# Attention with decay and a gated feed-forward: two groups of small matmuls move into the visits of their neighbours

## The chip, the cores and the metric

The kernel runs on one core of a Trainium2 chip. Its time is the device time of one execution in microseconds (us); the number that counts is the median of several runs. Five engines work side by side, each with its own queue that runs in order: PE (TensorE, matrix products; PEld is its weight load), DVE (VectorE), ACT (ScalarE), POOL (GpSimd) and SP (SyncE, which issues most of the DMAs). Engines wait for each other by semaphores. PE writes only to PSUM, which has eight banks; DVE and ACT read them.

## The reference: what is computed

For 4 batches and 8 heads, sequences of 768 tokens with 64 numbers each are worked in blocks of 64 tokens. Each block takes its own tokens' scores and a state that is carried from block to block; the result goes through a two-layer network with a cosine gate.

```python
for b in range(nb):                                   # 12 blocks of 64 tokens
    intra = einsum('bhic,bhjc->bhij', qb, kb) * Dmask # scores, decayed and causal
    intra = einsum('bhij,bhjd->bhid', intra, vb)      # values
    inter = einsum('bhid,bhde->bhie', qb * lam_pow, kv_state)   # carried part
    out[block] = intra + inter
    kv_state = lam_block * kv_state + einsum('bhsd,bhse->bhde', kb * rev_pow, vb)
h = x @ w_in                 # x: 3072 x 512, w_in: 512 x 2048
return (h * cos(h)) @ w_out  # w_out: 2048 x 512
```

## The kernel before, in words

**Tokens.** The 3072 tokens are 24 blocks of 128 tokens. Two blocks that stand at the same place of two batches make a pair. The first four blocks are done otherwise, as two "spans" of 256 tokens each, the beginnings of the first two batches. Then come pairs 2 to 11; pair 2, called the third pair here (its number is `SPANS`), is the first one, and it continues the sequences of the two spans. The decays are folded into scaled copies of q and v, so that a state is a plain running sum.

**A pair.** SP loads q, k and v. `prepare` scales q, copies k to bf16 (both into the tile qk) and scales v (v_s). q and k are transposed into qkT, for the third pair on PE (L374) with copies by DVE (L377), for later pairs by DMA (L380). Then `add_scores` plans the scores (L422; DVE multiplies them by a mask into s_m, L427) and the update of the state (L434, in PSUM as ps_kv). `state` (L440) adds the update of each half of a block to the running sum, on DVE, and `state_16` (L445) makes the bf16 copy S on ACT; for the third pair the first sum is written as bf16 at once by DVE. `add_stretch` plans the values (L484, in PSUM as ps_o) and, onto the same bank, the carried part, which multiplies S by the transposed q (L516). Copies out of ps_o give xT (L524), the input of the network.

**Values in two groups.** For a block, the values come from four products of 64x64. `values` emits the first 16 matmuls of a pair (the crosswise ones), `values_carried` the other 16 and then the carried part. Both groups write the same places of PSUM from different row halves of the array[...]. Pairs in `APART` use other banks. Where the next pair's scores and update lie in between, a 1x1 DVE copy (`turn`, L501) reads the first group's result and the second group waits for it. The third pair has neither, and `values_carried` puts a PE drain between the groups:

```python
if not more and not apart:
    nc.tensor.drain()
```

**The spans' state.** `add_span_state` makes the running sum that both spans leave behind: 32 matmuls (L705), a copy from PSUM by DVE (L709), a bf16 copy by POOL (L712). The third pair needs it: the first half of its carried part reads the bf16 copy (the second half reads S), and its S is this sum plus its own update.

**The network.** `add_ffn` plans for each tile of tokens (4, 2, 2, 2, 2, 2, 2, 4 and 4 blocks, `TILES`) the hidden matmuls (L738, ps_h), the cosine on ACT (L744), the product on DVE (L750, g), the output matmuls (L784, ps_f, in fours of 0.216 us each), the copy out on ACT (L798) and the store on SP (L805 for the spans' tokens, L807 after). The weights w_out come in four parts through POOL's DMA queue (L268).

**The order.** Nothing here is ordered by hand. Every step is a `Task` with an engine, an assumed duration, the tasks it depends on and a priority; `Planner.order` plays them forward and gives each engine's order and the PSUM banks. A task's `then` makes another one follow it at once on its engine; scores and update of most pairs are tied like this, for the third pair they aren't (`early`). Tasks with `LATE` (30.0) as priority are taken when little else can start.

Of the kernel before, what the change touches and what calls it, by code (L numbers as in the profile page):

```python
# [18 lines left out]
SPANS = 2  # L19
# [13 lines left out]
OUTS = [{"qT": ("ACT", "ACT"), "kT": ("ACT", "ACT")}, {"qT": ("ACT", "ACT"), "kT": ("ACT", "ACT")}]  # L33
VALUES_OUT = [("ACT", "ACT"), ("DVE", "ACT")]
STATE_OUT = [("ACT", "ACT"), ("ACT", "ACT")]
LATE = 30.0
ORDER = "q0 k0 q1 k1 v0 v1 i0 i1 i2 i3 i4 i5 o0 o1 o2 q4 q5 k4 k5 o3"

W_IN = [2, 2, 2, 4, 4, 2]
# [104 lines left out]
def kernel(  # L144
# [10 lines left out]
    nc = tc.nc  # L155
# [89 lines left out]
    SW = 0.11  # L245
    halves = [slice(i * D, (i + 1) * D) for i in range(2)]
    live = {}
# [4 lines left out]
    def prio_attn(n, part):  # L252
        i = next(i for i in range(len(TILES)) if n < first[i + 1])
        return begins[i - 1] + unit[i - 1] * (n - n % 2 - first[i] + 2 * part) / TILES[i]
# [146 lines left out]
    def new_sum(pr, half):  # L401
        t = live["sum", pr, half] = toks.tile([P, H, D], F32, tag=f"sum{half}", bufs=1 + half, name=f"sum{half}")
        return t
# [66 lines left out]
        qk_head[pr].frees = [T[pr, 0], T[pr, 1], u]  # L470
        return s_t, u

    def add_stretch(pr):

        n0 = 2 * pr
        g, c = divmod(pr, NB)
        pa = lambda part: prio_attn(n0, part)
        tile_i, j0 = tile_of(n0)

        def value(s, half, o=None):  # L480
            m = halves[half]
            o = live["o", n0 + s][:, :, m] if o is None else o
            for h in range(H):
                yield lambda h=h: nc.tensor.matmul(  # L484
                    o[halves[h % 2], h // 2], lhsT=live["v_s", n0 + s][m, h, :], rhs=live["s_m", n0 + s][m, h, :],
                    start=(apart or s != half) and h < 2, stop=True, skip_group_check=True)

        def values(t):
            for s in range(2):
                live["o", n0 + s] = bank(t.bank[s], [P, NP, P], F32, "ps_o")  # L490
            cross = [None, None]
            if apart:

                cross = live["cross", pr] = [bank(i, [P, NP, D], F32, "ps_x") for i in t.bank[2:]]
            for x, y in zip(value(1, 0, cross[0]), value(0, 1, cross[1])):
                x()
                y()

        def turn(_):

            live["turn", pr] = nc.vector.tensor_copy(spare[D:D + 1, 0:1], live["o", n0][D:D + 1, NP - 1, D:D + 1])  # L501

        def values_carried(_):
            if not more and not apart:
                nc.tensor.drain()
            for x, y in zip(value(0, 0), value(1, 1)):
                i = x()
                y()
                if ("turn", pr) in live:
                    tc.add_manual_dep(i.ins, live.pop(("turn", pr)).ins.name, mybir.DependencyInfo(  # L510
                        mybir.DependencyClass.Sync, mybir.DependencyReason.DATA), reason="row halves in turn")
            for half in range(0 if c else 1, 2):
                S = live["S", pr, 0] if half else live["S", pr - 1, 1]
                for h in range(H):
                    for s, r in enumerate(halves):
                        nc.tensor.matmul(live["o", n0 + s][halves[h % 2], h // 2, halves[half]], lhsT=S[r, h, :],  # L516
                                         rhs=live["qkT", pr][r, 0, h, halves[half]],
                                         start=False, stop=True, skip_group_check=True)

        def values_out(_, s, e):  # L520
            if ("xT", tile_i) not in live:
                live["xT", tile_i] = work.tile([P, KD, 4 * P], BF16, tag="xT", name="xT")
            j = j0 + s
            (nc.vector.tensor_copy if e == "DVE" else nc.scalar.copy)(  # L524
                live["xT", tile_i][:, :, j * P:(j + 1) * P], live.pop(("o", n0 + s)))

        def halves_out(_, s, half):
            if ("xT", tile_i) not in live:
                live["xT", tile_i] = work.tile([P, KD, 4 * P], BF16, tag="xT", name="xT")
            o, i = live["o", n0 + s][:, :, halves[half]], (j0 + s) * P + half * D  # L530
            x = live["xT", tile_i][:, :, i:i + D]
            if s == half:
                nc.scalar.copy(x, o)
            elif half or c:
                nc.vector.tensor_add(x, o, live["cross_f", pr][half])  # L535
            else:
                nc.vector.tensor_copy(x, live["cross_f", pr][half])

        def cross_out(_, half):
            live.setdefault(("cross_f", pr), {})[half] = toks.tile([P, NP, D], F32, tag=f"cross{half}", bufs=1, name=f"cross{half}")  # L540
            nc.scalar.copy(live["cross_f", pr][half], live["cross", pr][half])

        deps = [So[n0], So[n0 + 1], Uo[pr, 0], Uo.get((pr - 1, 1)) if c else None]
        more = pr + 1 < NBLK // 2 and pr + 1 not in ALONE
        apart = pr in APART
        v1 = pl.add("PE", 4 * QUART + SW, deps, values, pa(0.5), banks=2 + 2 * apart)
        chain = [v1]
        if more:
            nxt = list(add_scores(pr + 1, pa(0.5)))
            for t in nxt:  # L550
                v1.deps += [d for d in t.deps if d not in nxt]
            chain += nxt
        if more:
            deps = deps + [pl.add("DVE", 0.12, [v1], turn, pa(-9.0))]
        v2 = v12[pr] = pl.add("PE", (12 if c else 8) * QUART + (0.0 if more or apart else 0.28), deps, values_carried, pa(0.5))
        chain.append(v2)
        v1.bank_frees = []
        if apart:
            after = [v2] + ([h_last[tile_i - 2]] if tile_i >= 2 else [])
            copies = [pl.add("ACT", 0.42, after, partial(halves_out, s=s, half=s), pa(0.6)) for s in range(2)]  # L560
            moved = [pl.add("ACT", 0.42, [v1], partial(cross_out, half=half), pa(0.55)) for half in range(2)]
            sums = [pl.add("DVE", 0.4, after + [moved[1 - s]], partial(halves_out, s=s, half=1 - s), pa(0.0 if pr == SPANS else 0.59 - 0.01 * s)) for s in range(2)]
            for s in range(2):
                Vo[n0 + s] = [copies[s], sums[s]]
            v1.bank_frees = [Vo[n0], Vo[n0 + 1], [moved[0]], [moved[1]]]
        for s in range(2):
            So[n0 + s].frees = [v2]
            v_head[n0 + s].frees = [v2]
            if apart:
                continue  # L570
            e = "DVE" if pr == SPANS and s == 0 else "ACT"
            Vo[n0 + s] = [pl.add(e, 0.65, [v2] + ([h_last[tile_i - 2]] if tile_i >= 2 else []), partial(values_out, s=s, e=e),
                                 pa(0.0 if e == "DVE" else 0.6))]
            v1.bank_frees.append(Vo[n0 + s])
        qkT_head[pr].frees = [v2]
        if (pr + 1, 1) in Uo:
            Uo[pr + 1, 1].deps.append(v2)
        for x, y in zip(chain, chain[1:]):
            x.then = y
            y.deps.append(x)  # L580
# [113 lines left out]
        L["update"], L["values"], L["carried"] = u, v0, second  # L694
        L["straight"] = v1

    def add_span_state():


        def update(t):  # L700
            live["kv", 1] = bank(t.bank[0], [P, H, D], F32, "ps_kv")
            for h in range(H):
                for s in range(2):
                    for L, r in zip(spans, halves):
                        nc.tensor.matmul(live["kv", 1][r, h, :], lhsT=L["k"][:, s, h, :], rhs=L["v"][:, s, h, :],  # L705
                                         start=(h == 0 and s == 0), stop=True, skip_group_check=True)

        def state(_):
            nc.vector.tensor_copy(new_sum(1, 1), live["kv", 1])  # L709

        def state_16(_):
            nc.gpsimd.tensor_copy(new_S(1, 1), live["sum", 1, 1])  # L712

        u = pl.add("PE", 16 * QUART + SW, span_deps + [w_t["out", 0]], update, LATE, banks=1)
        x = pl.add("DVE", 0.69, [u], state, LATE)
        Uo[1, 1] = pl.add("POOL", 0.61, [x], state_16, LATE)
        u.bank_frees = [[x]]

    h_last, o_last = {}, {}
# [120 lines left out]
    idle = pl.add("SETUP", 0.0, [], None, -1e9, banks=1)  # L840
    for x in range(SPANS):
        add_span(x)
    add_span_state()
    for pr in range(SPANS, NBLK // 2):
        prepare(pr)
    add_scores(SPANS, prio_attn(2 * SPANS, 0.2))
    pr = SPANS
    for i in range(len(TILES)):
        while 2 * pr < first[i + 1]:
            if pr + 1 in ALONE:  # L850
                add_scores(pr + 1, prio_attn(2 * pr + 2, 0.2))
            add_stretch(pr)
            pr += 1
        add_ffn(i)
    for f in range(2, SPLIT):
# [60 lines left out]
```

## Time and profile before

| | |
|---|---|
| median of 5 runs | 204.26 us (204.19 to 204.32) |
| profiled execution, its own time | 204.56 us |
| its span, first to last instruction | 202.9 us |
| granted TensorE clock | 0.999 |
| PE busy, share of the span | 97% |
| DVE, ACT, POOL busy | 58%, 59%, 32% |
| moved by DMA | 33.94 MB, mean 167 GB/s |

The span is what the trace sees; the execution's own time has 1.66 us more around it. The page gives for each engine its busy time, and the chain that ended last: from the last instruction back, at each step to what released it or to the instruction before it on its engine. The timeline lists instructions in order of start, runs of the same kind merged; the duration of such a run reaches from the first start to the last end, and in brackets stands how long the engine was idle before it and what ended that.

### The profile page before, as it was taken

The page shows a single profiled execution, that of the slowest core. Times are in us where ns is not written, and L with a number is a line of the kernel's source. Part 1 is how long each engine was busy: PE and PEld are TensorE (multiplying, and loading weights), DVE is VectorE, ACT ScalarE, POOL GpSimd, SP SyncE. Part 2 cuts the span into 40 slices and gives each one's busy share as a digit, 9 for nine tenths or more (in the row PEclk, how much of TensorE's full clock was granted, in tenths as well). Part 3 has the DMA queues.
Part 4 walks back from the last instruction along what each step waited for, and adds up shares of the span by engine and source line. Part 5 has one row for each costly group of instructions (what it writes and reads, how often), then busy time and mean ns, then how long its engine had stood idle before and what let it go on. Part 6 is the DMA issues. An engine that isn't in the chain of part 4 may idle for free.

```text
span 202.9 us, 5941 instructions
## 1 busy us (share of the span) xinstructions
PE 196.7 (97%) x2469; PEld 116.6 (57%) x2469; DVE 116.8 (58%) x228; ACT 120.0 (59%) x240; POOL 64.7 (32%) x85
## 2 busy tenths in 40 slices
PE   6799999999999999999999999999999999999994
PEld 3367444547847848666658676755445444444443
DVE  2888774256954967848548675734579544444001
ACT  4978872128837878565639667653877655355120
POOL 5694004046145163643733364552620000000000
PEclk9999999999999999999999999999999999999999
DMA  4999999979889998999999999999940010111112
GB/s 118 323 190 205 203 202 220 195 162 226 192 218 232 244 217 190 225 120 273 239 246 181 169 278 210 247 145 238 249 113 3 3 52 0 52 55 52 52 52 103
DMA packets 96762, 33.94 MB, mean 167 GB/s; under 512 B 84320, under 2 KB 93792, under 8 KB 96736
## 3 DMA queue, kind: packets, MB, share of 16 engines
q1 hardware_dynamic: 89232, 28.78, 63.4%
q0 software_dynamic: 7360, 4.72, 16.3%
q8 instruction: 19, 0.31, 0.6%
q10 hardware_dynamic: 144, 0.07, 0.1%
q14 instruction: 7, 0.06, 0.1%
HBM read 27.27 MB, written 6.29 MB: 165 GB/s over the span
## 4 chain that ended last, share of the span: by engine, by line
PE 93%; DMA 3%; SPq 2%; POOL 1%; issue 0%; ACT 0%; POOLq 0%; ACTq 0%
PE ps_h L738 42%; PE ps_f L784 41%; DMA sp_f<-in_k_dram 3%; PE ps_kv L434 2%; PE ps_o L484 2%; PE ps_s L422 2%; PE ps_o L516 2%; SPq L268 1%; PE ps_o L644 1%; PE ps_kv L631 1%; POOL k_sp L599 1%; PE ps_x L484 0%; PE ps_t L374 0%; PE ps_t L607 0%; PE ps_s L618 0%; PE ps_o L650 0%
## 5 line engine op out<-in xcount | busy, mean ns | idle before, releaser
L750 DVE TENSOR_TENSOR g<-ps_h,cos 128x256 bf16<-128x256 f32 (+1 forms) x148 | 73.2, 503 | 42.8 <-ACT cos L744 42.0
L744 ACT ACTIVATE cos<-ps_h,halfpi 128x256 f32<-128x256 f32 (+1 forms) x148 | 75.7, 539 | 29.4 <-PE ps_h L738 28.6
L784 PE MATMUL ps_f<-w_out_sb,g 128*128 128x512 bf16 (+2 forms) x400 | 91.5, 371 | 0.0
L738 PE MATMUL ps_h<-xT,w_in_sb 128*128 128x256 bf16 (+1 forms) x592 | 91.3, 304 | 0.0
L738 PEld LDWEIGHTS <-w_in_sb 128*128 128x128 bf16 x592 | 57.1, 98 | 30.1 <-DVE xT L524 0.4
L784 PEld LDWEIGHTS <-g 128*128 128x128 bf16 x400 | 37.6, 98 | 37.2
L798 ACT COPY o_sb<-ps_f 128x512 f32<-128x512 f32 (+1 forms) x24 | 13.8, 573 | 30.4 <-PE ps_f L784 30.3
L344 POOL TENSOR_TENSOR qk<-q_f,q_scale 128x512 bf16<-128x512 f32 x19 | 19.6, 1045 | 35.0 <-DMA q_f<-in_q_dram 28.4
L352 POOL TENSOR_TENSOR v_s<-v_f,v_scale 128x512 bf16<-128x512 f32 x19 | 19.6, 1044 | 16.2 <-DMA v_f<-in_v_dram 16.2
L427 DVE TENSOR_TENSOR s_m<-ps_s,mask 128x512 bf16<-128x512 f32 x20 | 13.0, 685 | 3.6 <-PE ps_s L422 3.1
L348 POOL CAST qk<-k_f 128x512 bf16<-128x512 f32 x18 | 11.1, 614 | 12.7 <-DMA k_f<-in_k_dram 12.5
L524 ACT CAST xT<-ps_o 128x512 bf16<-128x512 f32 x11 | 6.0, 588 | 9.6 <-PE ps_o L516 6.2
L440 DVE TENSOR_TENSOR sum<-sum,ps_kv 128x512 f32<-128x512 f32 x15 | 10.2, 681 | 0.6
L445 ACT CAST S<-sum 128x512 bf16<-128x512 f32 x15 | 9.2, 617 | 0.9 <-DVE sum L440 0.8
L798 DVE COPY o_sb<-ps_f 128x384 f32<-128x384 f32 x1 | 0.6, 558 | 11.5 <-DMA out_dram<-o_sb 11.5
L484 PEld LDWEIGHTS <-v_s 64*64 64x64 bf16 x320 | 3.9, 107 | 4.1 <-issue 3.6
L876 PE MATMUL ps_idle<-blank 128*128 128x512 f32 (+2 forms) x8 | 4.7, 725 | 1.6 <-DVE blank L211 1.6
L623 DVE TENSOR_TENSOR s_m_sp<-ps_s,mask_sp 128x512 bf16<-128x512 f32 x8 | 5.1, 684 | 1.0 <-PE ps_s L618 1.0
L484 PE MATMUL ps_o<-s_m,v_s 64*64 64x64 bf16 x256 | 5.1, 196 | 0.1
L712 POOL CAST S<-sum 128x512 bf16<-128x512 f32 x1 | 0.6, 608 | 14.0 <-DVE sum L709 14.0
L501 DVE COPY spare<-ps_o 1x1 f32<-1x1 f32 x5 | 0.8, 156 | 7.3 <-PE ps_o L484 7.3
L535 DVE TENSOR_TENSOR xT<-ps_o,cross 128x256 bf16<-128x256 f32 x8 | 3.1, 422 | 2.9 <-PE ps_o L516 2.9
(74 smaller groups left out, 95.4 us busy)
## 6 DMA issues: line engine op xcount, KB each, us to landing
q_f<-in_q_dram SPq DMA_DIRECT2D x20, 256.0 KB, 4.2
k_f<-in_k_dram SPq DMA_DIRECT2D x20, 256.0 KB, 4.4
v_f<-in_v_dram SPq DMA_DIRECT2D x20, 256.0 KB, 5.0
out_dram<-o_sb SPq DMA_DIRECT2D x19, 256.0 KB, 3.4
w_out_sb<-in_moe_w_out_dram POOLq DMA_DIRECT2D x4, 512.0 KB, 12.6
sp_f<-in_q_dram SPq DMA_DIRECT2D x2, 512.0 KB, 6.3
sp_f<-in_k_dram SPq DMA_DIRECT2D x2, 512.0 KB, 5.7
w_in_sb<-in_moe_w_in_dram POOLq DMA_DIRECT2D x4, 256.0 KB, 6.9
```

The costliest lines, as they stand in the source:

```text
L344: vec[e].tensor_mul(new_qk()[:, 0, :, s], live.pop(("q_f", 2 * pr + s)), q_scale[:, c, :].unsqueeze(2).to_broadcast([P, H, D]))
L348: (nc.scalar.copy if early else nc.gpsimd.tensor_copy)(new_qk()[:, 1, :, s], live.pop(("k_f", 2 * pr + s)))
L352: vec[e].tensor_mul(live["v_s", 2 * pr + s], live.pop(("v_f", 2 * pr + s)), v_scale[:, c, :].unsqueeze(2).to_broadcast([P, H, D]))
L427: nc.vector.tensor_mul(t, live["s", pr][s], mask.unsqueeze(1).to_broadcast([P, H, D]))
L440: nc.vector.tensor_add(new, live["sum", pr, 0] if half else live["sum", pr - 1, 1], live["kv", pr][half])
L445: nc.scalar.copy(new_S(pr, half), live["sum", pr, half])
L484: yield lambda h=h: nc.tensor.matmul(o[halves[h % 2], h // 2], lhsT=live["v_s", n0 + s][m, h, :], rhs=live["s_m", n0 + s][m, h, :], start= ...
L738: nc.tensor.matmul(t[:, :n], lhsT=w_in_sb[:, kd, f * P:(f + 1) * P], rhs=live["xT", i][:, kd, at], start=(kd == 0), stop=(kd == KD - 1))
L744: nc.scalar.activation(c[:, :n], live["h", i, f, at.start][:, :n], AF.Sin, bias=halfpi)
L750: return nc.vector.tensor_mul(live["g", i][:, f, at], live.pop(("h", i, f, at.start))[:, :n], live.pop(("c", i, f, at.start))[:, :n])
L784: nc.tensor.matmul(live["f", i, j, piece][:, :width], lhsT=live["g", i][:, f, j * P:(j + 1) * P], rhs=w_out_sb[:, f, part], start=(f == 0) ...
L798: (nc.scalar.copy if eng == "ACT" else nc.vector.tensor_copy)(o[:, :width], live["f", i, j, piece][:, :width])
```

## The change: what it does

The spans' state update is tied in front of the third pair's scores (`u.then = s_t`), with their priority instead of `LATE`; its copy out of PSUM goes from DVE to ACT. The third pair's first group of values is tied in front of that pair's state update (`v1.then = ahead`), and takes the update's dependencies as well as those on the scores. In `values_carried` the third pair loses the drain and gets the 1x1 copy (`turn`) to wait for. For all later pairs the plan is made by the same lines as before.

On the engines this gives the following. PE, between the hidden matmuls of the first tile and those of the second, before: 32 of the spans' update; 24 output matmuls; 8 transposes; 8 output; 8 transposes; 8 output; 32 scores; 16 output; 32 of the update; 4 output; 32 values with a drain in the middle; 32 carried; 4 output. After: 28 output; 8 transposes; 8 output; 8 transposes; 8 output; 32 of the spans' update; 32 scores; 12 output; 16 values; 32 of the update; 4 output; 16 values; 32 carried; 4 output. DVE loses the copy of the spans' sum and gets the 1x1 copy behind its scaling of v. ACT gets the spans' sum between its last k copy and its first output copy. POOL's bf16 copy moves behind its first scaling of v. On SP two output stores of later tiles change places with one q load each.

```diff
-LATE = 30.0
...
-    def add_stretch(pr):
+    def add_stretch(pr, ahead=None):
...
         def values_carried(_):
-            if not more and not apart:
+            if not more and not apart and not ahead:
                 nc.tensor.drain()
...
-        v1 = pl.add("PE", 4 * QUART + SW, deps, values, pa(0.5), banks=2 + 2 * apart)
-        chain = [v1]
+        if ahead:
+            v1 = pl.add("PE", 4 * QUART + SW, [So[n0], So[n0 + 1]] + ahead.deps, values, ahead.prio, banks=2)
+            v1.then = ahead
+            ahead.deps.append(v1)
+            chain = []
+        else:
+            v1 = pl.add("PE", 4 * QUART + SW, deps, values, pa(0.5), banks=2 + 2 * apart)
+            chain = [v1]
...
-        if more:
+        if more or ahead:
             deps = deps + [pl.add("DVE", 0.12, [v1], turn, pa(-9.0))]
-        v2 = v12[pr] = pl.add("PE", (12 if c else 8) * QUART + (0.0 if more or apart else 0.28), deps, values_carried, pa(0.5))
+        v2 = v12[pr] = pl.add("PE", (12 if c else 8) * QUART + (SW if ahead else 0.0), deps, values_carried, pa(0.5))
...
-    def add_span_state():
+    def add_span_state(s_t, prio):
...
         def state(_):
-            nc.vector.tensor_copy(new_sum(1, 1), live["kv", 1])
+            nc.scalar.copy(new_sum(1, 1), live["kv", 1])
...
-        u = pl.add("PE", 16 * QUART + SW, span_deps + [w_t["out", 0]], update, LATE, banks=1)
-        x = pl.add("DVE", 0.69, [u], state, LATE)
-        Uo[1, 1] = pl.add("POOL", 0.61, [x], state_16, LATE)
+        u = pl.add("PE", 16 * QUART + SW, span_deps + s_t.deps, update, prio, banks=1)
+        u.then = s_t
+        s_t.deps.append(u)
+        x = pl.add("ACT", 0.61, [u], state, prio)
+        Uo[1, 1] = pl.add("POOL", 0.61, [x], state_16, prio)
...
-    add_span_state()
...
-    add_scores(SPANS, prio_attn(2 * SPANS, 0.2))
+    first_scores, first_update = add_scores(SPANS, prio_attn(2 * SPANS, 0.2))
+    add_span_state(first_scores, prio_attn(2 * SPANS, 0.2))
...
-            add_stretch(pr)
+            add_stretch(pr, first_update if pr == SPANS else None)
```

## The prediction, made before the changed kernel ran

> **What bounds the kernel now.** I read the page first: its busy shares and the engines of the chain that ended last.
>
> ```profile
> PE 196.7 (97%) x2469; PEld 116.6 (57%) x2469; DVE 116.8 (58%) x228; ACT 120.0 (59%) x240; POOL 64.7 (32%) x85
> PE 93%; DMA 3%; SPq 2%; POOL 1%; issue 0%; ACT 0%; POOLq 0%; ACTq 0%
> ```
>
> TensorE is on the chain for 93% of the span, and no other engine is above 59% busy. So the time is the length of PE's queue plus what PE stands still, and an edit is worth what it takes off that. All edits lie between 30 and 47 us, so next I read the chain in order of time there (start us, us, what):
>
> ```profile
> 30.11 0.62 PE ps_kv L705 x32
> 30.74 5.29 PE ps_f L784 x24
> ...
> 40.37 0.38 PE ps_s L422 x32
> 40.74 3.56 PE ps_f L784 x16
> 44.30 0.55 PE ps_kv L434 x32
> 44.85 0.97 PE ps_f L784 x4
> 45.82 0.25 PE ps_o L484 x16
> 46.07 0.10 issue
> 46.17 0.32 PE ps_o L484 x16
> 46.49 0.28 PE ps_o L516 x32
> 46.77 0.97 PE ps_f L784 x4
> ...
> 56.48 0.38 PE ps_s L422 x32
> 56.86 0.37 PE ps_kv L434 x32
> 57.23 3.56 PE ps_f L784 x16
> ```
>
> Four times PE leaves the wide output matmuls (ps_f, 128 rows by 128 columns of the array) for small attention matmuls: the spans' state update (L705), the scores (L422), the state update (L434), and the values with the carried part (L484, L516). I call each excursion a visit. The return costs too: 24, 16 and 4 output matmuls at 0.216 us are 5.18, 3.46 and 0.86, and the chain has 5.29, 3.56 and 0.97, so 0.10 to 0.11 more on every return. The visits therefore cost (0.62+0.11) + (0.38+0.10) + (0.55+0.11) + (0.25+0.10+0.32+0.28+0.11) = 2.93 us.
>
> Then the timeline, for array shapes and for what the visits wait on (start us, us, engine, line, operation, tiles, array shape):
>
> ```profile
> 14.51 0.62 PE L631 MATMUL ps_kv<-v_sp,k_sp 64*128 64x128 bf16 x8
> 15.06 0.42 PE L644 MATMUL ps_o<-s_m_sp,v_sp 64*64 64x128 bf16 x16
> ...
> 40.30 0.45 PE L422 MATMUL ps_s<-qkT 64*64 64x64 bf16 x32
> 42.77 1.04 POOL L352 TENSOR_TENSOR v_s<-v_f,v_scale 128x512 bf16<-128x512 f32 x1 [7.41 <-DMA v_f<-in_v_dram]
> 43.38 0.98 DVE L352 TENSOR_TENSOR v_s<-v_f,v_scale 128x512 bf16<-128x512 f32 x1 [1.22 <-DMA v_f<-in_v_dram]
> 44.23 0.61 PE L434 MATMUL ps_kv<-v_s,qk 64*64 64x64 bf16 x32
> 44.89 0.69 DVE L440 TENSOR_TENSOR S<-sum,ps_kv 128x512 bf16<-128x512 f32 x1 [0.53 <-PE ps_kv L434]
> ```
>
> The 32 scores take 0.45 us, the 32 matmuls of the update 0.61. The difference, 0.16, is a stall just after the update's start: its third matmul needs the scaled values that DVE finishes at 43.38+0.98 = 44.36, and those were held by the landing of v_f. The transfer sets this moment, not PE.
>
> **The change, part by part.**
>
> Part A, spans' update into the scores' visit. One return (0.11) and one entry go. What stands in the way is the shape: L705 uses 128*64, the scores 64*64. The Trainium skill (TensorEngine Tiling (Array Packing), section Tiling Modes) says that changing the tiling mode, unlike changing the tile, drains the array; that speaks against the gain. The trace has no 128*64 next to 64*64; the nearest row is L631 (64*128) followed by L644 (64*64): eight matmuls 0.057 apart from 14.51 end their starts at 14.91, and the next starts at 15.06, 0.15 later, 0.09 more than their spacing. Groups of one shape follow each other without it: in other visits 32 scores behind values take 0.26 on the chain (at 104.97). By the rule, scores behind the spans' update cost 0.26 + 0.10 = 0.36; without it 0.26. A is then 0.62+0.36+0.11 = 1.09 against 0.73+0.48 = 1.21: saves 0.12, or 0.22 if this pair of shapes doesn't drain. I take 0.12.
>
> Moved with it: the copy of the span state from PSUM goes from DVE (0.69) to ACT and the bf16 copy on POOL (0.61) comes later. ACT is free: between its two k copies (the last ends at 35.79+0.62 = 36.41) and its first output copy at 43.48 it has nothing, so 0.61 at about 41.0 hides there. On POOL the bf16 copy now stands behind the scaling of v at 42.77 to 43.81, so it ends at 44.42 and holds the next q scaling (44.32 before) by 0.1; POOL idles 0.46 us two operations later (k copy at 46.82, waiting for its load), so this ends there. Its reader, the first half of the carried matmuls, comes at about 46.0: 1.6 us of cover. No load changes its place in POOL's or SP's queue; the last w_out part on POOL waits for q_f and is issued at 33.54 either way. Late on SP two output stores move ahead of one q_f load each (near 90 and 135 us); the copy that feeds the first had ended at 88.42, and the second by 135.02, so neither waits.
>
> The 24 output matmuls of the chain at 30.74 become 28, start 0.72 earlier, and the 16 at 40.74 become 12: no matmul is added or lost. DVE is 0.69 freer at 30.8, where it is ahead of need.
>
> Part B, the first 16 value matmuls into the update's visit. Values first 0.25 (like 45.82), then the update at the price it has behind another group (0.29 at 70.26; 0.37 at 56.86, the upper end), and 0.11 for the return: 0.65, against 0.66 with its stall and 0.50 without. So B adds 0.15 of PE work.
>
> Part C, second values and carried part alone. The drain (0.10 issue, and 0.32 instead of 0.25 for the second group's restart) and the first group go: 0.25+0.28+0.11 = 0.64 against 1.06, saves 0.42; with carried at 0.34, as at 61.16, 0.36. In the drain's place the second values wait for a 1x1 DVE copy (L501, 0.16 us in its group's row) that reads the first values' result. It stands in DVE's queue between the v scaling and the S addition. The update and four output matmuls, some 1.2 us, lie between the first and the second values, so it is covered; uncovered it would cost about 0.3, what the drain costs.
>
> Sum without stalls in the changed kernel: 2.93 − (1.09+0.65+0.64) = 0.55 us.
>
> **Where the stall goes.** Before B PE does the same work less A's 0.12, so it stands ready at 44.23−0.12 = 44.11. But the first value matmul already reads the DVE-scaled v, which ends at 44.36, and PE takes up such a release some 0.05 later (xT ends at 46.85+0.69 = 47.54, its matmul starts at 47.60). PE waits from 44.11 to 44.41: 0.30. Behind it in PE's queue stand the update and the output matmuls, and for the update DVE's S addition. B's own work is 0.15 longer, so S comes at about 45.05 instead of 44.89 and ends at 45.75; the second half of the carried matmuls is at about 46.2. Net 0.55 − 0.30 = 0.25 us. A's gain is thus lost in the stall (whichever way the shape switch goes), and the rest is C less B.
>
> If v were scaled in time, the kernel before would lose its 0.16 stall too, and the gain would be 0.55−0.16 = 0.39, or 0.49 without a switch. That may be so outside the profile: the profiled execution took 204.56, the median of the runs is 204.26. With the dearer update and carried rows the gain is 0.25−0.14 = 0.11. So the gain lies between 0.11 and 0.49; I take 0.25, from the trace's own timing. Against the profiled execution: 202.9 of span + 1.66 around it = 204.56, becomes 204.31 (span 202.65); carried to the median, 204.26−0.25 = 204.01.
>
> **The rivals.**
>
> *Absorbed later.* At 92.60 PE waits for transposes that a DMA brings:
>
> ```profile
> 92.60 0.33 PEld L422 LDWEIGHTS <-qkT 64*64 64x64 bf16 x32 [0.31 <-DMA qkT<-qk]
> ```
>
> The array ends its last matmul's stream about 0.1 us sooner than it can start here (other entries from ps_h idle 0.21). SP is issuing back to back from 77 us until these transposes are out at 90.1, so they would not come earlier with PE, and all of the gain would turn into this wait: 204.26. Against it: the five runs lie within 0.13 us, narrow for a kernel hanging on one transfer, and DMA moved only 9 GB/s between 88 and 90 us, a pause that other runs need not have.
>
> *v in time.* The gain is 0.39 to 0.49, 203.77 to 203.87. For it: the 0.30 us between profile and median. Against: a load of a saturated queue (169 to 234 GB/s from 34 to 42 us) has no evident reason to land sooner.
>
> *Slower: w_out's third part late.* Output matmuls start 0.72 earlier. The thirteenth needs the third part of w_out at 30.67+12x0.216−0.72 = 32.54; issued at 16.74 with the longest landing of its group, 15.4, it is there at 32.1. Cover is 0.4. If it lands after 32.54, PE stops for the excess; the first 0.30 of that is taken from the stall at 44.1, the next 0.25 eats the gain, and from 33.1 on the kernel is slower. A landing at 33.6 gives 204.76. The narrow spread of the runs speaks against 1.0 us of scatter.
>
> *The change does nothing:* excluded, since the instruction order shows three visits for four and no drain.
>
> **How the numbers follow.** What a measurement can tell from no change is about 0.2%, 0.41 us: faster is below 203.85, slower above 204.67. Chances: 0.47 for the likeliest (own range 203.90 to 204.15), 0.20 absorbed (204.15 to 204.35), 0.23 v in time, 0.10 slower. Faster takes the larger part of v in time and the low tail of the likeliest, where several small prices fall together: 0.30. Slower: 0.10. Same: the rest, 0.60. The range leaves out the far end of the slower case and the extreme of v in time: 203.78 to 204.33.
>
> **What would show it.** In the changed profile: one entry from wide matmuls to L711 near 40.4 with the scores behind it, some 0.1 us after its last matmul (switch) or at once; PE idle before the first values until v_s at about 44.4; the S addition at about 45.05; no issue gap inside the third visit; the next hidden matmuls at about 47.35 instead of 47.60; then an equal queue 0.25 earlier up to 92 us, where the wait on qkT is about 0.1, gone, or grown by 0.25. Wrong would make me: v scaled well before 44.1, a price for two shapes in one visit beyond 0.15, a wait on the 1x1 copy, or a stall among the first output matmuls.

## The result, and the profile after

The changed kernel takes 203.83 us (median of 36 runs), the kernel before 204.23 us (71 runs beside it). The ratio is 0.9978, with a 95% interval of 0.9971 to 0.9986: between 0.29 and 0.59 us less. The medians lie 0.40 us apart, where 0.25 was forecast. Four single runs of the experiments below fell in a slow state of the chip and took 3 to 5 us longer than the rest of their kernel; they are left out of the medians and ranges given.

The page of the changed kernel, its busy times and the engines of the chain that ended last:

```profile
PE 196.6 (97%) x2469; PEld 116.6 (58%) x2469; DVE 116.1 (57%) x228; ACT 120.5 (60%) x241; POOL 64.6 (32%) x85
PE 93%; DMA 3%; SPq 2%; POOL 1%; issue 0%; ACT 0%; POOLq 0%; ACTq 0%
```

TensorE is still the bound, with the same 2469 matmuls. The chain of the changed kernel in order of time (start us, us, what) shows the three visits:

```profile
30.06 6.04 PE ps_f L792 x28
...
40.45 0.62 PE ps_kv L711 x32
41.07 0.38 PE ps_s L421 x32
41.45 2.70 PE ps_f L792 x12
44.15 0.25 PE ps_o L484 x16
44.39 0.26 PE ps_kv L433 x32
44.65 0.97 PE ps_f L792 x4
45.62 0.25 PE ps_o L484 x16
45.87 0.28 PE ps_o L516 x32
46.16 0.97 PE ps_f L792 x4
47.12 7.02 PE ps_h L746 x64
```

There is no issue row between the last two small groups, and the update, which took 0.55 us before, takes 0.26. The hidden matmuls begin at 47.12 on the chain, where the kernel before had its last four output matmuls begin at 46.77 and run until 47.74.

The timeline of the changed kernel has what the forecast was about, the scaled v and the first values (start us, us, engine, line, operation, tiles, idle time before it and what ended it):

```profile
42.84 0.80 DVE L351 TENSOR_TENSOR v_s<-v_f,v_scale 128x512 bf16<-128x512 f32 x1
43.04 1.07 POOL L718 CAST S<-sum 128x512 bf16<-128x512 f32 x1
44.08 0.32 PE L484 MATMUL ps_o<-s_m,v_s 64*64 64x64 bf16 x16
44.45 0.16 DVE L501 COPY spare<-ps_o 1x1 f32<-1x1 f32 x1 [0.81 <-PE ps_o L484]
44.80 0.69 DVE L439 TENSOR_TENSOR S<-sum,ps_kv 128x512 bf16<-128x512 f32 x1 [0.20 <-ACT o_sb L806]
...
91.82 0.33 PEld L421 LDWEIGHTS <-qkT 64*64 64x64 bf16 x32 [0.21 <-issue]
```

DVE has v ready at 42.84 + 0.80 = 43.64, and the first values start at 44.08, when PE gets there: nothing waits. The last line is the visit that waited for transposes at 92.60 before. It comes at 91.82, and its idle time of 0.21 is that of an ordinary entry.

From matmul start to matmul start, the visits can be priced without the modelled ends. The excess of a visit is the time from the last wide matmul before it to the first one after it, less one pitch of 0.216 us:

| visit | before | after |
| --- | --- | --- |
| spans' update | 0.720 | |
| scores (after: with the spans' update) | 0.471 | 1.095 |
| state update (after: behind the first values) | 0.640, of which 0.169 is the stall for v | 0.604 |
| values and carried part | 1.042 | 0.629 |
| sum | 2.873 | 2.328 |

Together 0.545 less: 0.376 of structure, and 0.169 that was a stall of the profiled execution of before. Its PE ends 0.772 earlier in all. The other parts are a start 0.053 earlier, 0.074 that the update at 56.9 waited before and not after, and 0.099 at the transposes near 92 us. The difference of the medians, 0.40, is close to the structure alone. (The visits leave out 0.012 by which the wide matmuls between them run closer together; with it the structure is 0.388.)

### The profile page after: what moved, and what is told of

The parts are those of the page before. It is cut to its first block, busy times and chain, and to the rows that moved or that the text cites. A ratio compares the mean times of both kernels' runs of the same rounds, so it can differ in the third digit from the quotient of the medians.

```text
span 202.1 us, 5941 instructions
## 1 busy us (share of the span) xinstructions
PE 196.6 (97%) x2469; PEld 116.6 (58%) x2469; DVE 116.1 (57%) x228; ACT 120.5 (60%) x241; POOL 64.6 (32%) x85
## 4 chain that ended last, share of the span: by engine, by line
PE 93%; DMA 3%; SPq 2%; POOL 1%; issue 0%; ACT 0%; POOLq 0%; ACTq 0%
PE ps_h L746 42%; PE ps_f L792 42%; DMA sp_f<-in_k_dram 3%; PE ps_o L484 2%; PE ps_s L421 2%; PE ps_o L516 2%; PE ps_kv L433 1%; SPq L267 1%; PE ps_o L650 1%; PE ps_kv L637 1%; POOL k_sp L605 1%; PE ps_x L484 0%; PE ps_t L373 0%; PE ps_t L613 0%; PE ps_s L624 0%; PE ps_o L656 0%
## 5 line engine op out<-in xcount | busy, mean ns | idle before, releaser
L267 POOL DMA_DIRECT2D w_out_sb<-in_moe_w_out_dram x4 | 3.0, 784 | 15.9 <-DMA q_f<-in_q_dram 15.9
```

## The experiments

To compare kernels whose starts differ by hundredths, I use one length from each trace: from the start of the last hidden matmul ahead of the output matmuls near 30 us to the start of the first hidden matmul near 47 us. It is 17.864 in the profile of before and 17.307 in both profiles of the changed kernel. Without its stall, before would have 17.695; that this is right shows in a run below without the stall, which has 17.868 with a copy that costs 0.169 more than the drain.

**Theory T**: the gain is a sum of terms in PE's queue, and v is in time in most executions. **Rival R1**: it is all the drain, and A is worth nothing. **Rival R2**: most of it is the timing of transfers that an earlier PE happens to meet.

### The parts alone

Part A without B and C (against the changed kernel; the drain is then kept):

```diff
-            add_stretch(pr, first_update if pr == SPANS else None)
+            add_stretch(pr)
```

> Part A alone: the spans' state update stands ahead of the scores of the third pair, with the copy on ACT; update and values stay as before, drain included. Theory T (the gain is PE's queue, term by term): one entry and one return go, one change of array shape comes, so PE has about 0.10 us less to do; where v is scaled late, the state update's stall takes it back. Gain 0 to 0.10: 204.13 to 204.23. Rival R1 (the drain is all of it, the shape change eats what the joint visit saves): 204.23. Rival R2 (the gain is mostly timing of loads and transposes that an earlier PE happens to meet): any number up to 0.4, with the wait for transposes near 92 us gone. In the trace T expects 0.12 to 0.13 from the last start of the spans' update to the first of the scores, and 0.10 less from the first visit to the update's.

Measured: 204.09 us against 204.24, ratio 0.9987 (0.9977 to 0.9997). Its length is 17.589, 0.106 below 17.695.

Parts B and C without A (against the changed kernel; priority, engine and place of the spans' update are those of before):

```diff
...
-        u = pl.add("PE", 16 * QUART + SW, span_deps + s_t.deps, update, prio, banks=1)
-        u.then = s_t
-        s_t.deps.append(u)
-        x = pl.add("ACT", 0.61, [u], state, prio)
+        u = pl.add("PE", 16 * QUART + SW, span_deps + [w_t["out", 0]], update, LATE, banks=1)
+        x = pl.add("DVE", 0.69, [u], state, LATE)
```

> Parts B and C alone: the first 16 value matmuls ahead of the state update, the 1x1 copy in the drain's place; the spans' update stays in its own visit with its copy on DVE. T: B adds 0.13, the drain and the moved group take off 0.41, so 0.28 less, or 0.26 where v is scaled late: 203.95 to 203.97. R1: 203.83, all of the gain. R2: nearer to 204.23, since the queue up to 44 us keeps its timing. In the trace T expects values and update 0.022 apart, and no gap in the visit of second values and carried part.

Measured: 204.00 us, ratio 0.9994 (0.9981 to 1.0008). Single times run from 203.87 to 205.01, so the interval alone decides nothing. The length does: 17.415, 0.280 below.

> The changed kernel once more, on the chip that runs the parts. T: A and BC add up to it, 0.36 to 0.40 below the kernel before, 203.83 to 203.87, with the first values waiting for the scaled v in some executions only. R2: the distance differs from the sum of the parts by over 0.1.

Measured: 203.86 us, ratio 0.9986 (0.9974 to 0.9998), length 17.307. The chains of A alone and of B and C alone, in that order, each at its second and third visit:

```profile
44.12 0.38 PE ps_kv L433 x32
44.50 0.97 PE ps_f L792 x4
45.47 0.25 PE ps_o L484 x16
45.71 0.10 issue
45.82 0.32 PE ps_o L484 x16
46.13 0.28 PE ps_o L516 x32
```

```profile
44.53 0.25 PE ps_o L485 x16
44.78 0.26 PE ps_kv L434 x32
45.04 0.97 PE ps_f L791 x4
46.01 0.25 PE ps_o L485 x16
46.26 0.29 PE ps_o L517 x32
```

With A alone the drain's row and the longer restart are there; with B and C they are gone. The lengths add up: 0.106 + 0.280 = 0.386 against 0.388 for both. The medians do too: 0.15 + 0.24 = 0.39 against 0.38. R1 falls, since A gains by itself: its interval just excludes 1, and the length says it more firmly. R2 falls as the main cause: the whole gain is in the lengths before 47.1 us, and of nine profiles of kernels with 2469 matmuls only that of before waits near 92 us.

### The drain against an uncovered copy

The kernel before, with the 1x1 copy where the drain stood:

```diff
             if not more and not apart:
-                nc.tensor.drain()
+                turn(_)
```

> The kernel before with the drain replaced by the 1x1 copy, nothing moved: the copy lies between the two groups of values with nothing over it. From the trace: 0.23 to 0.25 us from the last start of a small group to the start of a DVE operation behind it, 0.16 for the copy, about 0.07 back to PE: 0.46 to 0.48 from group to group, where the drain has 0.29. T: 0.15 to 0.2 slower than before, 204.38 to 204.43; the prediction's own text gave an uncovered copy the price of the drain, 204.23. R1 in its strong form (the copy is simply cheaper than the drain, the moved groups add nothing): 203.95 or less.

Measured: 204.41 us against 204.24, ratio 1.0013 (1.0001 to 1.0025). Its chain at that visit:

```profile
45.66 0.28 PE ps_o L484 x16
45.95 0.02 issue
45.97 0.17 DVE spare L501
46.14 0.04 issue
46.18 0.32 PE ps_o L484 x16
```

From the last start of the first group to the first of the second it is 0.461 us, where the drain has 0.292: an uncovered copy is 0.17 dearer than the drain, and so is the run. So it is not the copy that gains. It is free in the changed kernel only because an update and four output matmuls lie over it: 1.35 us pass between the two groups. For B and C, though, R1 is nearly right. The sixteen moved matmuls cost about as much in the update's visit (0.133) as they leave in their own, and what remains, 0.28, is about the drain's gap of 0.292.

The timeline of this kernel, which is the kernel before up to 45.6 us, also tells how usual the late v was:

```profile
42.88 0.76 DVE L352 TENSOR_TENSOR v_s<-v_f,v_scale 128x512 bf16<-128x512 f32 x1 [0.70 <-DMA v_f<-in_v_dram]
44.25 0.45 PE L434 MATMUL ps_kv<-v_s,qk 64*64 64x64 bf16 x32
```

v is scaled at 43.64, and the update takes 0.45, not 0.61. In seven other profiles the scaling starts between 42.76 and 42.96. The profile of before, with 43.38, was the odd one: its v_f landed at 43.36, in these eight between 42.63 and 42.94.

### A v that is surely late

Both kernels with DVE's scaling of this v done twice:

```diff
-            vec[e].tensor_mul(live["v_s", 2 * pr + s], live.pop(("v_f", 2 * pr + s)),
-                              v_scale[:, c, :].unsqueeze(2).to_broadcast([P, H, D]))
+            v_f = live.pop(("v_f", 2 * pr + s))
+            for _ in range(2 if e == "DVE" else 1):
+                vec[e].tensor_mul(live["v_s", 2 * pr + s], v_f,
+                                  v_scale[:, c, :].unsqueeze(2).to_broadcast([P, H, D]))
```

> The kernel before, in which DVE scales the v of the sixth block twice, the second time over the first. v is ready some 0.8 to 1.0 us later. T: the state update's third matmul waits for it, 0.2 to 1.1 us more than before by when v_f lands: 204.3 to 205.3. It is the base for the changed kernel with the same edit.

> The changed kernel with v scaled twice. T: now the first values surely wait for v, so part A's 0.10 and the missing stall vanish, and the rest is C less B: 0.25 to 0.28 below the kernel before with the same edit. R1 (A is worth nothing in any case): 0.36 to 0.40 below it. In the trace the first values start some 0.05 to 0.1 us after the second scaling ends.

Measured: 204.55 us (ratio to before 1.0022, 1.0004 to 1.0039) and 204.57 us (1.0009, 0.9989 to 1.0029). The single times run from 204.15 to 206.77 and from 204.24 to 205.25, so the times don't tell whether the second is faster. The traces do, for one execution each. The chain of the changed kernel with this edit:

```profile
42.88 0.61 DVE v_s L353
43.49 0.02 issue
43.51 0.99 DVE v_s L353
44.50 0.04 issue
44.54 0.32 PE ps_o L486 x16
44.86 0.26 PE ps_kv L435 x32
```

The first values start 0.05 us after the second scaling, as forecast for a late v. The lengths are 18.031 and 17.762: 0.269 apart instead of 0.388. So the step "A's gain is lost in the stall, and the rest is C less B" describes what happens where v is late. It only is not late.

### The copy's engine

The changed kernel with the span state's copy on DVE instead of ACT:

```diff
-            nc.scalar.copy(new_sum(1, 1), live["kv", 1])
+            nc.vector.tensor_copy(new_sum(1, 1), live["kv", 1])
```

> The changed kernel with the span state's copy back on DVE, in the place that its part of the queue gives it: ahead of the two products with the mask. T: these and the scaling of v come 0.2 us later, v is ready at 43.83 to 44.0 and PE stands ready at 44.08, so the time is the same as with ACT, 203.83 to 203.9. Rival: the move to ACT is part of the gain, PE then waits for v, 204.0 or more.

Measured: 203.82 us, ratio 0.9987 (0.9974 to 0.9999), length 17.308. Its timeline:

```profile
42.90 1.07 DVE L351 TENSOR_TENSOR v_s<-v_f,v_scale 128x512 bf16<-128x512 f32 x1
44.06 0.32 PE L484 MATMUL ps_o<-s_m,v_s 64*64 64x64 bf16 x16
```

v is ready at 43.97, some 0.1 before PE starts on it. The move to ACT is no part of the gain; it is a margin.

### Without the change of shape

The spans' update cut along its rows into 64 matmuls of 64*64, the shape of the scores, each half of the rows in its own bank; ACT copies both banks, DVE adds them behind the scaling of v, and POOL's bf16 copy follows that:

```diff
                     for L, r in zip(spans, halves):
-                        nc.tensor.matmul(live["kv", 1][r, h, :], lhsT=L["k"][:, s, h, :], rhs=L["v"][:, s, h, :],
-                                         start=(h == 0 and s == 0), stop=True, skip_group_check=True)
+                        for m, kv in zip(halves, live["kv", 1]):
+                            nc.tensor.matmul(kv[r, h, :], lhsT=L["k"][m, s, h, :], rhs=L["v"][m, s, h, :],
+                                             start=(h == 0 and s == 0), stop=True, skip_group_check=True)
...
-            nc.scalar.copy(new_sum(1, 1), live["kv", 1])
+            part = live["part"] = toks.tile([P, H, D], F32, tag="part", bufs=1, name="part")
+            nc.scalar.copy(new_sum(1, 1), live["kv", 1][0])
+            nc.scalar.copy(part, live["kv", 1][1])
```

> The changed kernel with the spans' update cut along its rows into 64 matmuls of the array shape of the scores (64*64), each half of the rows in a bank of its own; ACT copies both, and DVE adds them behind the scaling of v. T: the shape change of 0.126 becomes an ordinary 0.022, and 64 matmuls at 0.008 take as long as 32 at 0.016: 0.08 to 0.10 less than the changed kernel, 203.73 to 203.76. If the gap is not from the shape, it stays 0.126 and the time 203.83. If the pace of the small matmuls does not hold over 64, the time is above 203.83.

Measured: 204.74 us against 204.19, ratio 1.0026 (1.0012 to 1.0040). In the visit the theory held for the gap: between the two groups it is 0.012 us from start to start, where the changed kernel has 0.126, and the 64 matmuls take 0.515 against 0.499. The scores take 0.290 instead of 0.252, which no run explains, so the length is 17.240, only 0.067 below the changed kernel, where 0.08 to 0.10 was expected. Later the kernel loses far more than that. The timeline of this kernel near 131 us:

```profile
130.60 0.93 PE L752 MATMUL ps_h<-xT,w_in_sb 128*128 128x256 bf16 x7
131.89 0.10 PEld L752 LDWEIGHTS <-w_in_sb 128*128 128x128 bf16 x1 [0.65 <-issue]
131.90 0.28 PE L752 MATMUL ps_h<-xT,w_in_sb 128*128 128x256 bf16 x1 [0.37 <-issue]
```

And the same eight matmuls in the repeat of the changed kernel:

```profile
130.56 1.04 PE L746 MATMUL ps_h<-xT,w_in_sb 128*128 128x256 bf16 x8
```

Seven matmuls run, the eighth comes 0.53 late, and the trace names nothing that it waited for. No profile of a kernel with 2469 matmuls has this gap. Was it an accident of the execution, something on DVE, POOL or in PSUM, or the 64 instructions (32 matmuls and their weight loads) that this kernel adds to PE's queue?

> The kernel of square once more. Its first run was 0.085 us ahead of the changed kernel at 47 us, as meant, and then lost 0.53 in the middle of eight hidden matmuls at 131.3 us, on a gap for which the trace names no releaser, and 0.15 at the entry at 128.0; the median was 204.74 with single times from 203.81 to 205.92. If that is an accident of the chip or the execution, this run is at 203.73 to 203.85. If it belongs to the program, the median is again near 204.7, and a gap without a releaser is again in the trace.

Measured: 204.68 us (203.87 to 205.41), ratio 1.0008 (0.9994 to 1.0023). The gap is there again, before the same matmul:

```profile
132.86 0.10 PEld L752 LDWEIGHTS <-w_in_sb 128*128 128x128 bf16 x1 [1.12 <-issue]
```

The changed kernel with 64 more instructions at its start, as idle matmuls of 64 columns:

```diff
+        if at < 2.0:
+            cols -= D
         while cols > 0:
-            n = min(cols, 4 * P)
+            n = min(cols, 4 * P if at > 2.0 else D)
```

> The changed kernel with the idle matmuls of the first microseconds cut from 3 into 19 with about the same columns in all: 64 more instructions in PE's queue before the work begins, as many as square adds, and nothing else. If what square loses comes from the place of later instructions in PE's queue (blocks of it are fetched by transfers: 19 packets of 16 KB on an instruction queue), pad loses it too: 204.3 to 204.9, with wide scatter. If it comes from what square adds on DVE, POOL or in PSUM banks, pad is at 203.83.

Measured: 208.35 us. Of this, 4.3 us are a late start that I had not meant: an idle matmul of 64 columns is two in the profile, 0.215 us each, so the last one starts at 9.5 us and not at 5.5. The total says nothing, but the place does; the timeline of pad:

```profile
134.90 0.93 PE L746 MATMUL ps_h<-xT,w_in_sb 128*128 128x256 bf16 x7
136.13 0.10 PEld L746 LDWEIGHTS <-w_in_sb 128*128 128x128 bf16 x1 [0.59 <-issue]
```

Seven and one, at the same matmul, in a kernel that is the changed one from 10 us on but for its place in the queue. Two more kernels put small bf16 matmuls at the start instead: 64 more instructions on the changed kernel, and 192 more on the cut update (256 in all). The edit of the first is shown, without the zeroed tile `nought` that it reads; the second has 100 in place of 34 and 512 in place of 1024.

```diff
+        if at < 2.0:
+            for i in range(34):
+                r = m = halves[i % 2]
+                at_c = slice(0, D)
+                nc.tensor.matmul(idle_ps[r, at_c], lhsT=nought[m], rhs=nought[m], start=True, stop=True, skip_group_check=True)
+            cols = 1024
```

> The changed kernel with 34 small bf16 matmuls in the place of one idle matmul of the first microseconds: again 64 more instructions ahead of the work, now without the delay of 4.3 us that pad brought to the start. Theory Q (the place of later instructions in PE's queue decides): the first transposes start as before, near 6.4 us, a gap without a releaser of 0.4 to 1.0 us comes among the hidden matmuls near 131 us, and the time is 204.3 to 204.9. If pad's gap came from its late start: 203.8 to 203.9 and no gap.

> The kernel of square with 192 more instructions among the idle matmuls of the start (100 small ones for two wide ones), so that all that follows the spans' update stands 256 instructions later in PE's queue than in the changed kernel[...]. Theory Q: the gap near 131 us goes, and what square won shows: 203.73 to 203.78, below both kernels. If each added instruction costs something by itself, or if square's loss came from DVE, POOL or PSUM: 204.5 or more.[...]

Measured: 206.97 us (206.07 to 208.19) and 206.51 us (205.96 to 207.28). Both starts were disturbed again. Loads and scalings end late from the first transposes on: PE is 1.2 and 1.9 us behind by 13 us, and 1.2 and 2.9 us at the third pair's transposes near 36 us. In the first, a late v and late transposes near 58 us cost 1.2 us more. So neither total can be used, and no version of the cut update beats the changed kernel. The place, in the timeline of the first and then of the second:

```profile
133.07 0.93 PE L748 MATMUL ps_h<-xT,w_in_sb 128*128 128x256 bf16 x7
135.61 0.10 PEld L748 LDWEIGHTS <-w_in_sb 128*128 128x128 bf16 x1 [1.90 <-issue]
```

```profile
133.57 1.04 PE L754 MATMUL ps_h<-xT,w_in_sb 128*128 128x256 bf16 x8
```

With 64 more the gap is there (four profiles of three programs), with 256 more it is not (one profile). So the gap depends on how many instructions stand ahead in PE's queue, not on the kernel's data flow. That it is the fetch of instructions is likely, but no run changes the fetch alone. For it speaks, first, that the page has a queue for them; its row for the cut update (queue, packets, MB, share of 16 engines) is

```profile
q8 instruction: 19, 0.31, 0.6%
```

which is 19 packets of 16 KB. Second, in each of the four profiles one of them ends shortly before PE goes on, and always by nearly the same time. In the records of the single packets this packet ends at 130.63, 131.56, 134.73 and 134.25 us in the four profiles (in the order above), and PE's next weight load starts 1.26, 1.29, 1.40 and 1.36 us later. The last matmul before the gap has no such tie: it starts anywhere from 0.53 us before the packet's end (the longest gap) to 0.82 after it (the shortest). Third, the visit before the gap, at 127.4 us in the cut update, has 128 small matmuls with a weight load each, 256 instructions in 1.4 us. The Trainium skill (Runtime: NRT & Kernel Launch, section Instruction fetch mechanics) says that instructions come in blocks of 16 KiB, or 256, the next one fetched while the current one runs, and that crossing a boundary is mostly hidden. By the page's figure the visit is one block long (an estimate); if the fetch is the cause, the crossing was not hidden here. What stays open is whether this gap makes all of the cut update's loss, 0.91 us in the medians, and its scatter: the profiles show 0.53 and 1.00 us of it. Matmul by matmul against the profile of the changed kernel, the first of them loses 0.11 more near 128 us and 0.1 in small steps before.

## Why the prediction was right or wrong

**Right: the bound and the sum without stalls.** It had 0.55 us; the visits' excess fell by 0.545. Both count the stall of before as gone. A was to save 0.12 and saved 0.096 in the profiles (0.106 alone); B was to add 0.15 and added 0.604 − 0.471 = 0.133; C was to save 0.42 and saved 0.413. That the sum is so close is in part luck: the misses in A and B, 0.02 each, cancel.

**Right: the change of shape has its price.** The estimate from the nearest row was 0.09 over the spacing; between 128*64 and 64*64 it is 0.126 where groups of one shape have 0.022, so 0.10. The cut update shows it from the other side: the gap went to 0.012 when the shape was the same, though 0.05 of that came back in longer scores and a longer update.

**Wrong: the step "Where the stall goes".** It took v's readiness, 44.36, from the one profile of before and set it against PE's 44.11: a wait of 0.30. In the profile after, v was ready at 43.64 and PE at 44.08, and the term measured 0. That v_f lands as late as 43.36 is what the profile of before has and eight others don't have. The argument given against the rival, that a load of a saturated queue has no evident reason to land sooner, asked the wrong question: the one landing was the exception. The sign of it stood in the numbers. The profiled execution took 0.30 us more than the median of the runs, and its stalls are of that size: 0.169 for v, 0.074 at 56.9, 0.099 at 92.6. The text named this as speaking for the rival, and still forecast with the stalls in. The rival "v in time" had the mechanism and the number: 0.39, against 0.40 in the medians. The measured time lies within the forecast's range because that range took in most of this rival, not because the step held. That a late v would swallow A's gain was right, as the scaling done twice shows.

**Wrong, without effect: the copy uncovered costs what the drain costs.** It is 0.17 dearer. The cover held, so nothing came of it.

**Right: what is hidden.** The spans' copy ran on ACT at 41.12; on DVE it was hidden too. The bf16 copy on POOL took 1.07 us instead of 0.61 and ended at 44.11, well before its reader at 45.70. The output matmuls never waited for the third part of w_out. Of the three outcomes named for the wait near 92 us, "gone" came true.

## What to carry to other kernels

Before a wait in a profile enters a forecast, compare the profiled execution with the median: if it is longer by about the sum of its stalls, forecast with the stalls out, and keep the stall as the rival. Price a detour of TensorE by what it consists of: here an entry from a wide matmul is 0.31 us from start to start against a pitch of 0.216, a return 0.12, a change of array shape 0.10, a drain between two groups 0.27, and these sums held to 0.01 us when the parts were run alone. Here a wait in a drain's place gained only because other work lay over it, and 64 more instructions in a full queue cost more, far from where they stood, than they saved.

## What the runs showed of the hardware that was not expected

With 64 more instructions in PE's queue, put in at the start or near 40 us, PE stands still for 0.5 to 1.8 us before one and the same matmul (near 131 us, or 135 where the start was late), and goes on 1.26 to 1.40 us behind the end of a packet of the instruction queue. With 256 more it doesn't stand still there. Where DVE's scaling of v and POOL's copy to bf16 run at the same time, the later one pays: with DVE first (six profiles), the scaling took 0.68 to 0.80 us and the copy 1.07 to 1.11; with POOL first by 0.09 us (the copy on DVE), the copy took 0.61 and the scaling 1.07.
